# Attention's last four steps: transposes into the banks of the scores, and one sum a step later

## The chip, the cores and the metric

The kernel runs on one core of a Trainium2 chip. The metric is the device time of one execution in microseconds (us); before the change it is 531.19 us, the median of three runs (530.88 to 531.22). Engines are named as in the profile: PE (matrix products and transposes), PEld (its weight loads), DVE (vector), ACT (scalar), POOL (GpSimd), SP (which issues most DMAs). PE's results go to PSUM, which the program lays out as eight banks of 128 x 512 float32 values.

## The reference

Two stages follow each other: an attention with a bias that a small network computes from positions, and a layer with three weight matrices whose products are joined by a maximum.

```
scores = q @ k.T / sqrt(64) + bias(positions)        # 4 batches, 8 heads, 576 x 576
attn   = exp(scores - max); attn = attn / (sum(attn) + 1e-9)
x      = (attn @ v) as 2304 tokens x 512
h      = max(x @ w1, x @ w2, x @ w3)                 # 2304 x 768
out    = h @ w_out                                   # 2304 x 512
```

## The kernel before

The order of instructions on every engine is the order in which the program writes them; nothing is reordered later, and the framework only adds the waits between engines. It does so by tiles: two accesses of one tile by different engines may be given a wait, accesses of different tiles are not.

**The attention's steps.** The attention works through 72 steps (`NSTEP`), each 128 rows of scores for two heads. A step `n` goes through a pipeline that is five steps deep. In step `n` PE makes the scores (`front`, tiles `s`, two tiles of two banks each), DVE adds the bias and takes the maximum (`shift`), and ACT makes the exponentials (`expo`, tile `e`). Two steps later POOL multiplies `e` by the reciprocal of the row sums (`norm`, line 332; the reciprocal `rc` is DVE's, line 328, once for two steps). Four steps later (`LAG`) `flip` lets PE transpose `e` in pieces of 64 columns into PSUM: sixteen transposes go to the two one-bank tiles `tp..._0` and `tp..._1` (`ps_t`, tag `t`, two buffers, so one step's pair fills both), and two more go to the tile `lp` (one bank, one buffer), one of them first of all and one last. Then `empty` copies: ACT takes `tp..._0` and `lp` (line 470), DVE takes `tp..._1` (line 474), into the SBUF tile `et`. The products of `et` with the values (line 400) go to the one-bank tile `pv` (one buffer); DVE copies a finished `pv` to the tiles `xb` at the start of the next step (`split_x`, line 420).

**The drain.** In steps 72 to 75 (`n >= NSTEP`) no new scores are made, and the steps only finish what is in the pipeline: four calls of `flip`, those of the last pair of units, whose names are `tp_5` to `tp_8` in the program. There the spare time of DVE and ACT serves the next stage: `late_x` is cut into pieces, and the main loop lets each step do one piece for `vector` and one for `scalar`. Its pieces are sums and differences of blocks of `xb` (`sum`, on DVE, line 553; t3 in two halves, then t2), roundings of such a block (`high`, a cast on ACT, line 578) and remainders (`low`, on DVE or on POOL, line 553). In step 75, and after it, t4 and the last products follow; the last ones go to the tile `pvlast`, which takes a buffer of tag `t`.

**The second stage** (`moe`, line 653) begins as soon as PE has made the last products of the attention. It is a long row of products of 128x128 by 128x384 (lines 665 to 667).

The PSUM pool in this stretch has four banks of tag `s` (two buffers of two banks), two of tag `t`, one of `lp` and one of `pv`.

Of the kernel before, what the change touches and what calls it, by code (L numbers as in the profile page):

```python
# [19 lines left out]
def kernel(  # L20
# [17 lines left out]
    NTQ = S // 128  # L38
    LB = 128 * NTQ
# [10 lines left out]
    def ps_s(name, tag="s"):  # L50
        return psums[-1].tile([128, 2, 512], F32, tag=tag, bufs=2, name=name)
# [7 lines left out]
    def ps_t(name):  # L59
        return psums[-1].tile([128, 512], F32, tag="t", bufs=2, name=name)  # L60
# [148 lines left out]
    NSTEP = len(sched)  # L209
    LAG = 4  # L210
# [4 lines left out]
    def step_of(pair, y):  # L215
        return ORDERS[units[2 * pair][0] % 2][y]

    class Attention:
# [122 lines left out]
        def flip(self, n):  # L341
            pair, y = fronts[n]
            which, t = step_of(pair, y)
            pool, e2 = self.pool, self.st.pop(n)["e"]
            if y == MIX:
                self.group(2 * pair + 1, 1)
                parts = [(2 * pair, GW, 0, LEFT), (2 * pair + 1, GW, LEFT, LEFT)]
            else:
                un = 2 * pair + which
                if y in (0, 2, 7):  # L350
                    self.group(un, int(y == 2))
                parts = [(un, 128 * (t % 2), 0, 128)]
            lp = psums[-1].tile([128, 128], F32, tag="l", bufs=1, name=f"lp{pair}_{y}")
            tps = [ps_t(f"tp{pair}_{y}_{r}") for r in range(2)]
            blocks = [(2 * c + h, S * h + 128 * c + LEFT * h) for h in range(2) for c in range(NTQ)]

            def turn(r, to, k0):
                p = slice(64 * r, 64 * r + 64)
                return nc.tensor.transpose(to, e2[p, k0:k0 + 128], ident[p, p])  # L359

            a = turn(0, lp[:, 0:64], LB)
            for i, (o, k0) in enumerate(blocks):
                turn(1, tps[1][:, 64 * o:64 * o + 64], k0)
                turn(0, tps[0][:, 64 * o:64 * o + 64], k0)
            b = nc.tensor.nop()
            tc.add_manual_dep(b.ins, a.ins.name, mybir.DependencyInfo(
                mybir.DependencyClass.Sync, mybir.DependencyReason.DATA), reason="two row tiles write one bank")
            turn(1, lp[:, 64:128], LB)
            out = []
            for r in range(2):  # L370
                src = tps[r].rearrange("p (c h q) -> p c h q", c=NTQ, h=2)
                un, c0 = parts[r if y == MIX else 0][0:2]
                c0 += 0 if y == MIX else 64 * r
                out.append([(self.et[un][0][:, :, :, c0:c0 + 64], src)])
            out.append([(self.et[un][1][:, c0:c0 + w], lp[:, r:r + w]) for un, c0, r, w in parts])
            return out
# [746 lines left out]
    with tc.manual_schedule():  # L1123
# [4 lines left out]
        n = 0  # L1128
# [147 lines left out]
        x0 = Blocks(0, xa, xa)  # L1276
# [14 lines left out]
        def late_x():  # L1291
            yield "vector"
            x0.sum("t3", 0)
            yield "vector"
            x0.sum("t3", 1)
            x0.high("t3")
            x0.sum("t2")
            yield "scalar"
            x0.high("b21")
            yield "vector"  # L1300
            x0.low("b21", nc.gpsimd)
            yield "scalar"
            x0.high("t2")
            yield "vector"
            x0.low("t3")
            yield "scalar"
            x0.high("b22")
            yield "vector"
            x0.low("b22", nc.gpsimd)

        BEHIND = {3: 1, 5: 1, 7: 2, 11: 1, 13: 2, 15: 1}
        ex, lx = Stream(early_x()), Stream(late_x())
        while n < NSTEP + LAG:
            more = []
# [72 lines left out]
```

## Time and profile before

| what | value |
|---|---|
| median of three runs | 531.19 us (530.88 to 531.22) |
| the profiled execution's own time | 531.41 us |
| its span (first to last instruction) | 529.6 us |
| PE busy | 520.9 us, 98% of the span |
| DVE, ACT, POOL busy | 437.1, 358.0, 261.6 us |
| DMA | 78.66 MB, mean 149 GB/s |
| drain of the attention, first transpose to first product of the next stage | 249.55 to 261.05 us |

The span is 1.8 us shorter than the execution that it is part of. A row of the timeline gives the start and the length of an instruction or of a run of equal ones, and in brackets how long its engine had been idle and which instruction ended that. PE's matrix products are pipelined: several are under way at once, so a row of several products ends later than the last one starts, and PE counts as busy in short gaps between two starts.

### The profile page before, as it was taken

How to read it: one execution, taken by the hardware profiler on the slowest of the kernel's cores; microseconds unless marked ns; L12 is line 12 of the kernel's file. 1: busy time of each engine (PE TensorE's matmuls, PEld its weight loads, DVE VectorE, ACT ScalarE, POOL GpSimd, SP SyncE). 2: the span in 40 equal slices, each digit the busy share in tenths (PEclk: the TensorE clock that was granted, in tenths of full speed). 3: DMA queues.
4: the chain of work that ended last, by engine and by line, in shares of the span. 5: the costliest groups of instructions: out<-in, count | busy, mean ns of one | idle time of the engine just before them, and what ended most of it. 6: DMA issues, size and time to landing. Idle time of an engine off the chain costs nothing.

```text
span 529.6 us, 13653 instructions
## 1 busy us (share of the span) xinstructions
PE 520.9 (98%) x5175; PEld 434.1 (82%) x5175; DVE 437.1 (83%) x931; ACT 358.0 (68%) x803; POOL 261.6 (49%) x291
## 2 busy tenths in 40 slices
PE   8999999999999999999999999999999999999997
PEld 4454667676767676767799999999999999999997
DVE  7999979898989898988898998648887346898883
ACT  7998989998989999988685343442434325455552
POOL 0003878678878897987600074645665525300000
PEclk9999999999999999999999999999999999999999
DMA  6895998533675183211102225342275440756642
GB/s 188 256 340 150 318 286 239 163 108 109 214 227 152 25 244 120 68 24 38 67 0 81 79 70 179 131 160 79 80 251 170 145 141 11 249 178 179 198 143 80
DMA packets 73474, 78.66 MB, mean 149 GB/s; under 512 B 23168, under 2 KB 54528, under 8 KB 73408
## 3 DMA queue, kind: packets, MB, share of 16 engines
q1 hardware_dynamic: 73264, 77.49, 47.0%
q8 instruction: 41, 0.67, 0.5%
q10 hardware_dynamic: 144, 0.29, 0.2%
q14 instruction: 25, 0.20, 0.1%
HBM read 49.56 MB, written 27.94 MB: 146 GB/s over the span
## 4 chain that ended last, share of the span: by engine, by line
PE 90%; DVE 5%; ACT 2%; issue 1%; DMA 1%; DVEq 0%; ACTq 0%
PE pv L400 16%; PE p L667 12%; PE p L666 12%; PE p L665 12%; PE s L294 11%; PE tp L359 6%; PE p_o L1048 4%; PE p_o L1047 4%; PE p_o L1046 4%; PE bp L138 4%; DVE hid L116 3%; ACT e L318 2%; PE lp L359 2%; PE s L284 2%; DVE sn L304 1%
## 5 line engine op out<-in xcount | busy, mean ns | idle before, releaser
L332 POOL TENSOR_SCALAR e<-e,rc 128x576 f32<-128x576 f32 x144 | 111.6, 794 | 28.2 <-DVE rc L328 22.9
L304 DVE CUSTOM_DVE_ANT_0 sn<-s,bias 128x576 f32<-128x576 f32 x144 | 103.2, 754 | 22.1 <-PE lp L359 12.1
L318 ACT ACTIVATE e<-sn,nm 128x576 f32<-128x576 f32 x144 | 111.4, 780 | 4.6 <-DVE nm L304 4.4
L400 PE MATMUL pv<-et,vt 128*64 128x320 f32 (+1 forms) x496 | 74.0, 419 | 0.1
L359 PE MATMUL tp<-ident,e 64*128 64x64 f32 x1152 | 53.2, 224 | 0.5 <-ACT et L470 0.3
L474 DVE COPY et<-tp 128x512 f32<-128x512 f32 x72 | 49.3, 685 | 2.6 <-PE tp L359 2.5
L470 ACT COPY et<-tp 128x512 f32<-128x512 f32 x72 | 41.8, 581 | 12.4 <-PE lp L359 11.1
L294 PE MATMUL s<-kh,qh 64*128 64x288 f32 x240 | 48.3, 343 | 1.6 <-DVE nm L304 1.5
L359 PEld LDWEIGHTS tp<-ident,e 64*128 64x128 f32 x1152 | 47.4, 139 | 0.9 <-ACT et L470 0.4
L294 PEld LDWEIGHTS s<-kh,qh 64*128 64x128 f32 x240 | 28.1, 185 | 22.0 <-DVE nm L304 9.6
L400 PEld LDWEIGHTS pv<-et,vt 128*64 128x64 f32 x496 | 30.2, 136 | 17.8 <-issue 1.6
L707 ACT COPY u<-p 128x384 f32<-128x384 f32 x26 | 12.5, 481 | 43.4 <-PE p L667 43.3
L138 PE MATMUL bp<-hid,w2s 128*32 128x79 f32 (+51 forms) x640 | 40.4, 390 | 1.2 <-DVE hid L116 0.8
L294 PE MATMUL s<-kl,qh 64*128 64x288 f32 x240 | 41.0, 296 | 0.0
L294 PE MATMUL s<-kh,ql 64*128 64x288 f32 x240 | 39.9, 291 | 0.0
L116 DVE TENSOR_SCALAR hid<-sm,bp 128x528 f32<-128x528 f32 (+17 forms) x108 | 39.2, 447 | 0.0
L714 ACT COPY u<-p 128x384 f32<-128x384 f32 x26 | 12.5, 480 | 38.3 <-PE p L667 38.2
L138 PEld LDWEIGHTS bp<-hid,w2s 128*32 128x32 f32 x640 | 19.2, 109 | 22.9 <-issue 15.9
L553 POOL TENSOR_TENSOR ws<-wr 128x256 f32<-128x256 f32 x16 | 13.5, 844 | 47.9 <-DVE wl L553 47.5
L359 PE MATMUL lp<-ident,e 64*128 64x64 f32 x144 | 33.1, 230 | 1.1 <-ACT et L470 0.4
L553 DVE TENSOR_TENSOR q<-p,u 128x384 f32<-128x384 f32 x36 | 19.9, 554 | 15.7 <-ACT u L714 13.2
L359 PEld LDWEIGHTS lp<-ident,e 64*128 64x128 f32 x144 | 19.8, 137 | 13.6 <-issue 8.2
(236 smaller groups left out, 1627.5 us busy)
## 6 DMA issues: line engine op xcount, KB each, us to landing
bias_d<-bs SPq DMA_DIRECT2D x36, 295.5 KB, 5.1
w<-in_moe_w_dram SPq DMA_DIRECT2D x36, 256.0 KB, 3.1
bias<-bias_d SPq DMA_DIRECT2D x15, 576.0 KB, 5.5
h_d<-ht SPq DMA_DIRECT2D x18, 384.0 KB, 3.2
hin<-h_d SPq DMA_DIRECT2D x16, 384.0 KB, 4.4
qr<-in_qd_dram SPq DMA_DIRECT2D x16, 288.0 KB, 4.5
kr<-in_kd_dram SPq DMA_DIRECT2D x16, 288.0 KB, 5.3
vt<-in_v_dram SPq DMA_DIRECT2D x32, 128.0 KB, 3.3
```

The lines of the kernel that those rows point to most:

```text
L116: marks["hid"] = nc.vector.tensor_scalar(out=h[:, 0:n], in0=wl[:, 0:n], scalar1=k["bp"][:, m:m + 1], scalar2=0.0, op0=ALU.add, op1=ALU.max)
L138: nc.tensor.matmul(bp[32 * c:32 * c + 32, o:o + w], lhsT=w2s, rhs=src, start=True, stop=True)
L294: nc.tensor.matmul(ss[h][:, x, 0:HALF], lhsT=u[q][p, 128 * t:128 * t + 128], rhs=u[k][p, cols], start=(j == 0), stop=(j == len(terms) - 1))
L304: nc.vector.tensor_tensor_reduce(out=sn.rearrange("p (a b) -> p a b", a=2), in0=st["s"][h][:, :, 0:HALF], in1=bt.rearrange("p (a b) -> p a ...
L318: nc.scalar.activation(st["e"][:, S * h:S * h + S], sn, ACTF.Exp, scale=-1.0, bias=nm, accum_out=self.sm[:, x:x + 1])
L332: nc.gpsimd.tensor_scalar(out=e, in0=e, scalar1=self.rc[:, x:x + 1], scalar2=1.0, op0=ALU.mult, op1=ALU.mult)
L359: return nc.tensor.transpose(to, e2[p, k0:k0 + 128], ident[p, p])
L400: nc.tensor.matmul(pv[p], lhsT=w, rhs=x, start=(c == 0), stop=(c == NTQ))
L474: nc.vector.tensor_copy(*x)
L665: nc.tensor.matmul(o, lhsT=hi[:, c], rhs=h[:, j], start=first and j == 0, stop=False, **on)
L666: nc.tensor.matmul(o, lhsT=hi[:, c], rhs=l[:, j], start=False, stop=False, **on)
L667: nc.tensor.matmul(o, lhsT=lo[:, c], rhs=h[:, j], start=False, stop=last and j == 1, **on)
```

## The change

Two things are changed. In the four calls of `flip` whose step is one of the last four (`drain`), the two tiles of tag `t` are replaced by one tile of two banks from `ps_s`, of the tag that the scores use; its two buffers are taken in turn. In the same calls the first transpose into `lp` stands after the first eight of the other transposes (`NTQ` blocks of two) and no longer ahead of all. And in `late_x` the sum of t2 moves from the piece of the second half of t3 to the next piece for `vector`, behind the low part of b21.

```
@@ flip @@
             lp = psums[-1].tile([128, 128], F32, tag="l", bufs=1, name=f"lp{pair}_{y}")
-            tps = [ps_t(f"tp{pair}_{y}_{r}") for r in range(2)]
+            drain = n >= NSTEP - LAG
+            if drain:
+                tps = ps_s(f"tp{pair}_{y}")
+                tps = [tps[:, r] for r in range(2)]
+            else:
+                tps = [ps_t(f"tp{pair}_{y}_{r}") for r in range(2)]
...
-            a = turn(0, lp[:, 0:64], LB)
             for i, (o, k0) in enumerate(blocks):
+                if i == (NTQ if drain else 0):
+                    a = turn(0, lp[:, 0:64], LB)
                 turn(1, tps[1][:, 64 * o:64 * o + 64], k0)
                 turn(0, tps[0][:, 64 * o:64 * o + 64], k0)
@@ late_x @@
             x0.high("t3")
-            x0.sum("t2")
             yield "scalar"
             x0.high("b21")
             yield "vector"
             x0.low("b21", nc.gpsimd)
+            x0.sum("t2")
             yield "scalar"
             x0.high("t2")
```

**DVE in the drain.** The rows are DVE's program order from the copy of the `pv` of step 71 to the difference `t3l`. `tp_5` to `tp_7` are the transposed tiles of steps 72 to 74 (in the kernel before, the digit behind is the bank), `t_0` from `xb,xb` is the sum of t3, `t_0` from `t_0,xb` that of t2, and the brackets name the engines whose semaphore the instruction waits for. Before:

```order
L420 COPY xb_2_1179<-pv_0_5143 128x256
L474 COPY et_1_5234<-tp_5_1_5277 128x8x64 [waits PE_49]
L328 RECIPROCAL rc_5308<-sm_5213 128x4 [waits Activation_49,Pool_49]
L553 TENSOR_TENSOR t_0_5153<-xb_0_1172,xb_0_1169 128x384
L553 TENSOR_TENSOR t_0_5315<-t_0_5153,xb_0_1170 128x768 [waits DVE_49]
L474 COPY et_1_5234<-tp_6_1_5321 128x8x64 [waits PE_49]
L420 COPY xb_1_1175<-pv_1_5300 128x192 [waits PE_49]
L420 COPY xb_2_1179<-pv_1_5300 128x64 x2
L474 COPY et_0_5357<-tp_7_1_5360 128x8x64 [waits PE_49]
L553 TENSOR_TENSOR t3l_5390<-t_0_5153,t3h_5313 128x768 [waits DVE_49,Activation_49]
```

And after the change, the same stretch:

```order
L426 COPY xb_2_1179<-pv_0_5143 128x256
L480 COPY et_1_5234<-tp_5_5276 128x8x64 [waits Activation_49]
L328 RECIPROCAL rc_5307<-sm_5213 128x4 [waits Pool_49]
L559 TENSOR_TENSOR t_0_5153<-xb_0_1172,xb_0_1169 128x384
L480 COPY et_1_5234<-tp_6_5317 128x8x64 [waits Activation_49]
L559 TENSOR_TENSOR t_0_5348<-t_0_5153,xb_0_1170 128x768 [waits DVE_49]
L426 COPY xb_1_1175<-pv_1_5299 128x192 [waits PE_49]
L426 COPY xb_2_1179<-pv_1_5299 128x64 x2
L480 COPY et_0_5355<-tp_7_5357 128x8x64 [waits Activation_49]
L559 TENSOR_TENSOR t3l_5387<-t_0_5153,t3h_5312 128x768 [waits DVE_49]
```

The sum of t2 has changed places with the copy out of `tp_6`, and every copy out of a `tp` now names ACT where it named PE.

**PE in step 72.** The rows are PE's from the first transpose of the step to the first product into the next `pv`; before:

```order
L359 MATMUL lp_5_5275<-ident,e_5088 128x64 [waits Activation_49,Pool_49]
L359 MATMUL tp_5_1_5277<-ident,e_5088 128x64 [waits PE_49]
L359 MATMUL tp_5_0_5276<-ident,e_5088 128x64 [waits DVE_49]
...
L359 MATMUL lp_5_5275<-ident,e_5088 128x64 [waits PE_49]
L400 MATMUL pv_1_5300<-et_1_5112,vt_4917 64x320 [waits DVE_49,PE_49]
```

And after:

```order
L364 MATMUL tp_5_5276<-ident,e_5088 128x64 [waits DVE_49,Pool_49]
L364 MATMUL tp_5_5276<-ident,e_5088 128x64 x7
L364 MATMUL lp_5_5275<-ident,e_5088 128x64 [waits Activation_49,Pool_49]
L364 MATMUL tp_5_5276<-ident,e_5088 128x64 x8
L364 MATMUL lp_5_5275<-ident,e_5088 128x64 [waits PE_49]
L406 MATMUL pv_1_5299<-et_1_5112,vt_4917 64x320 [waits DVE_49,PE_49]
```

The wait for ACT, which is for the `lp` of the step before, stands behind eight transposes now, and the wait for DVE stands ahead of all and is for scores that DVE has read.

## Rows read from the trace of the kernel before

**Rows 1.** The page: each engine's busy time, share of the span, instructions

```profile
PE 520.9 (98%) x5175; PEld 434.1 (82%) x5175; DVE 437.1 (83%) x931; ACT 358.0 (68%) x803; POOL 261.6 (49%) x291
```

**Rows 2.** Busy time by stretches: stretch, length, engines, PEclk, DMA share, GB/s

```profile
262.00:290.00 28.00, 28.00 (x164) 28.00 (x163) 25.99 (x34) 19.99 (x34) 0.00 (x0) 1.00 0.12 38
```

**Rows 3.** Timeline of PE, the drain: start, length, engine, line, what, idle before

```profile
249.55 0.24 PE L359 MATMUL lp<-ident,e 64*128 64x64 f32 x1 [0.43 <-ACT et L470]
...
250.00 0.71 PE L359 MATMUL tp<-ident,e 64*128 64x64 f32 x15 [0.17 <-DVE et L474]
...
250.64 1.84 PE L400 MATMUL pv<-et,vt 128*64 128x320 f32 x12
252.41 0.27 PE L359 MATMUL lp<-ident,e 64*128 64x64 f32 x1
...
253.11 0.76 PE L400 MATMUL pv<-et,vt 128*64 128x320 f32 x4
...
254.34 0.27 PE L359 MATMUL lp<-ident,e 64*128 64x64 f32 x1
...
255.18 1.83 PE L400 MATMUL pv<-et,vt 128*64 128x320 f32 x12
...
257.65 0.76 PE L400 MATMUL pv<-et,vt 128*64 128x320 f32 x4
...
258.77 1.92 PE L400 MATMUL pvlast<-et,vt 128*64 128x256 f32 x16
...
261.05 0.44 PE L665 MATMUL p<-b11h,wh 128*128 128x384 f32 x1
```

**Rows 4.** Timeline of DVE, the drain

```profile
249.86 0.41 DVE L420 COPY xb<-pv 128x256 f32<-128x256 f32 x1
250.69 0.69 DVE L474 COPY et<-tp 128x512 f32<-128x512 f32 x1 [0.42 <-PE tp L359]
251.30 0.17 DVE L328 RECIPROCAL rc<-sm 128x4 f32<-128x4 f32 x1
251.39 0.53 DVE L553 TENSOR_TENSOR t<-xb,xb 128x384 f32<-128x384 f32 x1
251.95 1.38 DVE L553 TENSOR_TENSOR t<-t,xb 128x768 f32<-128x768 f32 x1
...
254.46 0.62 DVE L420 COPY xb<-pv 128x192 f32<-128x192 f32 x3 [0.53 <-PE pv L400]
...
255.70 2.29 DVE L553 TENSOR_TENSOR t3l<-t,t3h 128x768 fp32r<-128x768 f32 x1
...
260.42 0.95 DVE L553 TENSOR_TENSOR t<-xb,t 128x768 f32<-128x768 f32 x1
```

**Rows 5.** Timeline of ACT, the drain

```profile
249.01 0.40 ACT L470 COPY et<-lp 128x64 f32<-128x64 f32 x2
...
251.07 0.57 ACT L470 COPY et<-tp 128x512 f32<-128x512 f32 x1
...
251.95 0.83 ACT L578 CAST t3h<-t 128x768 fp32r<-128x768 f32 x1
252.69 0.83 ACT L578 CAST b21h<-xb 128x768 fp32r<-128x768 f32 x1
253.42 0.58 ACT L470 COPY et<-tp 128x512 f32<-128x512 f32 x1
253.90 0.27 ACT L470 COPY et<-lp 128x128 f32<-128x128 f32 x1
...
257.75 0.59 ACT L470 COPY et<-tp 128x512 f32<-128x512 f32 x1 [1.12 <-PE tp L359]
```

**Rows 6.** Timeline of POOL, the drain

```profile
247.73 2.92 POOL L332 TENSOR_SCALAR e<-e,rc 128x576 f32<-128x576 f32 x4 [1.24 <-DVE rc L328]
251.63 3.76 POOL L332 TENSOR_SCALAR e<-e,rc 128x576 f32<-128x576 f32 x4 [0.99 <-DVE rc L328]
255.35 1.83 POOL L553 TENSOR_TENSOR b21l<-xb,b21h 128x768 fp32r<-128x768 f32 x1
```

More of the change, by code (lines that the diff above doesn't have):

```diff
@@ L353, in flip @@
             lp = psums[-1].tile([128, 128], F32, tag="l", bufs=1, name=f"lp{pair}_{y}")
-            tps = [ps_t(f"tp{pair}_{y}_{r}") for r in range(2)]
+            drain = n >= NSTEP - LAG
+            if drain:
+                tps = ps_s(f"tp{pair}_{y}")
+                tps = [tps[:, r] for r in range(2)]
+            else:
+                tps = [ps_t(f"tp{pair}_{y}_{r}") for r in range(2)]
             blocks = [(2 * c + h, S * h + 128 * c + LEFT * h) for h in range(2) for c in range(NTQ)]
@@ L359, in turn @@
                 return nc.tensor.transpose(to, e2[p, k0:k0 + 128], ident[p, p])
-            a = turn(0, lp[:, 0:64], LB)
             for i, (o, k0) in enumerate(blocks):
+                if i == (NTQ if drain else 0):
+                    a = turn(0, lp[:, 0:64], LB)
                 turn(1, tps[1][:, 64 * o:64 * o + 64], k0)
@@ L1296, in late_x @@
             x0.high("t3")
-            x0.sum("t2")
             yield "scalar"
@@ L1301, in late_x @@
             x0.low("b21", nc.gpsimd)
+            x0.sum("t2")
             yield "scalar"
```

## The prediction

> **What bounds the kernel now.** The page comes first: PE is busy for 98% of the span [rows 1], so a change helps only where PE stands, and hurts only where it makes PE stand. Next the table by stretches, for what follows the attention: from 262 to 290 us PE is busy for 28.00 of 28.00 us, at a granted clock of 1.00 [rows 2], and the same view of the later stretches up to 500 us reads alike. So whatever moves the first product of the next stage, at 261.05, moves the end by as much; nothing behind it takes a gain or a loss back. Then the timeline of PE in the drain [rows 3]: PE stands for 0.43 us until ACT has copied the old `lp` and, two transposes later, for 0.17 us until DVE has copied the old `tp`. After that it hardly stands. The timelines of the other three engines [rows 4, 5, 6] show who is close behind PE there.
>
> From rows 3 I take PE's own pace: 1.77 us from the first of twelve `pv` rows to the next transposes (250.64 to 252.41), 1.23 us for eight (253.11 to 254.34), 0.70 us from the first transpose of an unstalled step to its products (252.41 to 253.11), and 1.12 us from the last eight `pv` rows to `pvlast` (257.65 to 258.77).
>
> **What the new banks give.** In step 72 the transposes no longer wait for DVE's copy. The wait for the old `lp` remains: ACT ends that copy at 249.01 + 0.40 = 249.41 [rows 5] and PE's `lp` began at 249.55, 0.14 later [rows 3]. It now holds back only the second eight transposes. In the kernel before, fifteen of them took from 250.00 to the products at 250.64; half of them take some 0.41, so PE would be ready at 249.96, 0.68 earlier. But the products go to the single `pv` bank, which DVE empties until 249.86 + 0.41 = 250.27 [rows 4]. With 0.08 for the wait the products begin at 250.35: a gain of 0.29 us, no more. At its own pace PE would begin step 73 at 252.12, its products at 252.82, step 74 at 254.05.
>
> **What the new tile costs.** The program's order shows that each DVE copy out of `tp` now waits for ACT, and the ACT instruction that reads the same tile is ACT's own copy of the other half. In the kernel before DVE copied at 250.69, ahead of ACT at 251.07 [rows 4, 5]. ACT's place doesn't change, since two exponentials and a small sum stand ahead of its copy. So DVE now starts at 251.07 + 0.57 + 0.03 = 251.67, that is 0.98 later (0.03 is what ACT takes to follow DVE: t3 ends at 251.39 + 0.53 = 251.92 and the cast of it starts at 251.95). Behind that copy in DVE's queue stand the reciprocal (now 252.28) and t3 (now 252.37 to 252.90). Two engines wait for these:
>
> - ACT's cast of t3, then its cast of b21, then its copies of step 73. They start at 251.95, 252.69, 253.42 and 253.90 [rows 5]; each is 0.98 later, the `tp` copy from 254.40 to 254.98, the `lp` copy to 255.15.
> - POOL's normalization, whose four pieces started 0.16 us behind the reciprocal [rows 4, 6]. They now start at 252.61; undisturbed, four take 2.92 instead of 3.76 [rows 6], and with t3 beside the first they end at some 255.68. No transpose is late by that.
>
> Step 74's transposes start at 254.05, and the second eight wait for the `lp` copy: 255.15 + 0.14 = 255.29, so PE is ready for the next `pv` at 255.70. Before, these products began at 255.18, just behind DVE's copies out of `pv` (254.46 + 0.62 = 255.08). Those copies are now later still. DVE's copy of step 73 waits for ACT's: 255.01 to 255.70. Then comes the moved sum of t2, from 255.63, and only then the copies out of `pv`.
>
> **The moved sum.** Its own length is 0.95 us, as the sum of equal shape at 260.42 shows; at 251.95 it took 1.38, with POOL's pieces beside it [rows 4, 6]. Its length in the new place is the unknown. The lower end is 0.95, the upper end a wait for all of POOL's b21 remainder (1.83, [rows 6]) with the sum behind it. Three rows tell how the two engines meet. At 251.95 DVE waited while POOL finished one piece, and went ahead of the next. The difference at 255.70 took 2.29 and ended at 257.99, 0.81 after POOL's remainder (255.35 + 1.83 = 257.18): again DVE stood for one POOL instruction and then ran at its own speed. So what matters is which is first. POOL's last piece ends at 255.68 and its remainder follows; DVE asks at 255.63, in time by 0.05. I take the lower end: the sum ends at 255.63 + 0.95 = 256.58.
>
> The Trainium skill says the same of this pair (SBUF — State Buffer, section SBUF: two separate sides): the shared port is an exclusive lock for a whole instruction, and the loser blocks. A split of bandwidth instead would stretch the sum to between 1.38 and 2.29 and give 534.0 to 534.9; the rows of 251.95 and 255.70 speak for the lock.
>
> **The sum.** The copies out of `pv` run from 256.50 to 257.12, and the last `pv` begins at 257.22 (0.10 behind, as before): 2.04 late. PE is at step 75 at 257.22 + 1.77 = 258.99, at its products at 259.69. ACT's copy starts 0.10 behind those (257.75 against 257.65, [rows 3, 5]), 259.79 to 260.38, and DVE's only then, 260.41 to 261.10. ACT and DVE are free by then: the cast of t2 starts at 256.61, ACT's copy of step 74 ends near 257.95, DVE's near 258.67, and the difference of t3 behind it near 259.54. `pvlast` needs both copies: at PE's pace it would begin at 259.69 + 1.12 = 260.81, but it waits until 261.10 + 0.06 = 261.16. Against 258.77 that is 2.39 us, of which 2.04 come from the queue around the moved sum and the rest from the two copies one after the other at the end. The tail of DVE behind `pvlast` shifts by no more than PE, so the next stage stays as it is.
>
> The profiled execution takes 531.41 us; 531.41 + 2.39 = 533.80. The runs' median lies 0.22 lower, so the forecast is 533.6 us.
>
> The Trainium skill speaks against any cost here (PSUM — Partial Sum Buffer, section Specifications (TRN2)): ScalarE and VectorE can read PSUM side by side at full rate when they use different banks. The two halves lie in two banks, so the chip would allow it; the rows of step 72, where DVE's copy (250.69 to 251.38) and ACT's (from 251.07) overlap, agree. By that rule the time would be that of the second rival below, and it doesn't apply if the program itself makes one wait for the other.
>
> **The rivals.**
>
> - *POOL is first.* If the remainder of b21 takes the port before t2, DVE stands until 255.66 + 1.83 = 257.49 and the sum ends near 258.30 (0.81 behind, as in the row of 255.70). All that follows is 1.7 later: 535.3 us. For it speaks the margin of 0.05 us, less than the latencies that I added up; against it, that DVE twice went ahead of a POOL instruction that was just starting.
> - *Not slower: the copies in effect run side by side.* If DVE's wait were met early, DVE would copy in step 72 before its reciprocal, which with t3 would stay at 251.30 and 251.39. It would copy step 73 from 252.89 to 253.58, t2 would run from 253.50 to 254.88 (at its old length of 1.38), the copies out of `pv` from 254.80 to 255.42, and the last `pv` would begin at 255.52, 0.34 late: 531.5 us, no change. It is decided at ACT's copy of step 72: ended by 250.6 it costs nothing, and all of its lateness beyond that counts. Against it: the wait in the program, and ACT's end at 251.64, which nothing in the change makes earlier.
> - *Faster.* All that PE loses to the old banks is the 0.68 us of step 72; with a free `pv` bank as well it would come through, and the time would be 530.5 us. That is still within 0.2%, so a clear gain would need a wait that I don't see.
>
> **How the numbers follow.** Forecast 0.61 (own range 533.0 to 534.4, from the latencies of some 0.05 us that add up over a dozen steps), POOL first 0.24 (534.9 to 535.7), no change 0.12, a clear gain 0.03. A measurement tells a difference of 0.2%, some 1.06 us, from none. So slower 0.85, same 0.12, faster 0.03. The range of 532.6 to 535.7 leaves out the last two cases and little else.
>
> **What would show it.** In the new profile: transposes of step 72 from near 249.1, its products near 250.35; DVE's copies each behind ACT's, the first near 251.67; ACT's `lp` copy of step 73 ending near 255.15 with PE waiting for it; the sum of t2 from near 255.63, of 0.95 us (or some 2.7 if POOL is first); the last `pv` near 257.2; `pvlast` near 261.2 behind DVE; the next stage near 263.4 and no idle PE in it. The forecast is wrong if DVE copies beside ACT, or if the copies out of `pv` start before 256 us.

## The result, and the profile after

The changed kernel takes 536.59 us (median of six runs, 536.24 to 538.54) against 531.13 us of the kernel before on the same chip: 1.0108 times as long, 95% interval 1.0098 to 1.0118. That is 5.46 us more, where 2.39 were forecast; the time lies 0.9 us above the range. The profiled execution took 537.24 us; its span is 535.5 us against 529.6. The next stage starts 6.09 us later, at 267.14 against 261.05, and from there both kernels run alike: PE is busy for all of the first 253 us in either. So the whole loss lies ahead of that stage.

The timeline of PE in the drain answers to [rows 3]; columns as there.

```profile
248.98 0.46 PE L364 MATMUL tp<-ident,e 64*128 64x64 f32 x8
249.48 0.24 PE L364 MATMUL lp<-ident,e 64*128 64x64 f32 x1
...
250.35 1.83 PE L406 MATMUL pv<-et,vt 128*64 128x320 f32 x12 [0.30 <-DVE xb L426]
...
255.21 0.24 PE L364 MATMUL lp<-ident,e 64*128 64x64 f32 x1 [0.62 <-ACT et L476]
...
258.81 3.47 PE L406 MATMUL pv<-et,vt 128*64 128x320 f32 x12 [3.02 <-issue]
262.20 0.79 PE L364 MATMUL tp<-ident,e 64*128 64x64 f32 x9
...
263.36 1.00 PE L406 MATMUL pv<-et,vt 128*64 128x320 f32 x4
...
264.83 1.95 PE L406 MATMUL pvlast<-et,vt 128*64 128x256 f32 x16
...
267.14 0.44 PE L671 MATMUL p<-b11h,wh 128*128 128x384 f32 x1
```

Step 72 starts 0.57 earlier, and its products 0.29 earlier than the 250.64 of before. Of both, 0.07 is no gain: this execution runs that much ahead before the change can act, as the first row of DVE below shows (249.79 against 249.86 in [rows 4]). The loss is in two places: PE stands for 3.02 us ahead of the last `pv`, and then the same twelve products take 3.39 us to the next transposes, where they took 1.76, from 255.18 in [rows 3] to this row of the kernel before:

```profile
256.94 0.27 PE L359 MATMUL lp<-ident,e 64*128 64x64 f32 x1
```

For the first place look at DVE; its timeline answers to [rows 4].

```profile
249.79 0.41 DVE L426 COPY xb<-pv 128x256 f32<-128x256 f32 x1
251.60 0.69 DVE L480 COPY et<-tp 128x512 f32<-128x512 f32 x1 [1.40 <-ACT et L476]
252.21 0.17 DVE L328 RECIPROCAL rc<-sm 128x4 f32<-128x4 f32 x1
252.30 0.52 DVE L559 TENSOR_TENSOR t<-xb,xb 128x384 f32<-128x384 f32 x1
254.94 0.69 DVE L480 COPY et<-tp 128x512 f32<-128x512 f32 x1 [2.12 <-ACT et L476]
255.54 2.63 DVE L559 TENSOR_TENSOR t<-t,xb 128x768 f32<-128x768 f32 x1
258.10 0.61 DVE L426 COPY xb<-pv 128x192 f32<-128x192 f32 x3
...
264.08 0.69 DVE L480 COPY et<-tp 128x512 f32<-128x512 f32 x1 [2.97 <-ACT et L476]
```

Every copy out of `tp` in the drain now ends an idle time with ACT's name behind it, and the sum of t2, the row of 128x768, takes 2.63 us instead of the 0.95 that was forecast. The timelines of ACT and of POOL, for [rows 5, 6], show who it waited for.

```profile
251.00 0.57 ACT L476 COPY et<-tp 128x512 f32<-128x512 f32 x1
...
254.32 0.58 ACT L476 COPY et<-tp 128x512 f32<-128x512 f32 x1
254.80 0.27 ACT L476 COPY et<-lp 128x128 f32<-128x128 f32 x1
...
263.46 0.59 ACT L476 COPY et<-tp 128x512 f32<-128x512 f32 x1 [3.04 <-PE tp L364]
```

```profile
252.57 3.02 POOL L332 TENSOR_SCALAR e<-e,rc 128x576 f32<-128x576 f32 x4 [2.00 <-DVE rc L328]
255.56 1.79 POOL L559 TENSOR_TENSOR b21l<-xb,b21h 128x768 fp32r<-128x768 f32 x1
```

ACT's copies end 0.03 ahead of DVE's (251.57 and 251.60, 264.05 and 264.08). POOL's remainder of b21 runs from 255.56 to 257.35, undisturbed, and t2 ends at 258.17, 0.82 behind it: DVE stood for the whole POOL instruction and then ran at its own speed.

The table by stretches has the second place: stretch, length, busy time of PE, PEld, DVE, ACT, POOL (in brackets the number of instructions), then PE's granted clock, the DMA share and GB/s.

```profile
255.80:257.00 1.20, 0.00 (x0) 0.00 (x0) 1.20 (x1) 0.00 (x0) 1.20 (x1) 1.00 0.00 0
257.00:258.80 1.80, 0.00 (x0) 0.02 (x1) 1.71 (x4) 0.59 (x1) 0.36 (x1) 0.52 0.00 0
258.80:260.00 1.20, 1.19 (x6) 0.67 (x8) 0.44 (x1) 1.20 (x4) 0.00 (x0) 0.50 0.00 0
260.00:262.00 2.00, 2.00 (x10) 0.69 (x6) 1.11 (x2) 0.42 (x1) 1.50 (x1) 0.50 0.00 0
...
263.00:264.00 1.00, 1.00 (x13) 0.61 (x12) 0.00 (x0) 0.54 (x2) 0.00 (x0) 0.56 0.00 0
264.00:265.00 1.00, 1.00 (x10) 0.37 (x8) 0.72 (x2) 0.22 (x2) 0.00 (x0) 1.00 0.00 0
...
267.00:290.00 23.00, 23.00 (x134) 22.86 (x133) 20.78 (x27) 17.16 (x28) 0.00 (x0) 1.00 0.08 24
```

PE ran at a granted clock of 1.00 (2.4 GHz), did nothing from 255.80, and soon after 257.00 the clock fell to 0.50 (1.2 GHz). It stayed there until almost 264, through the last twelve products and the transposes of step 75.

| from, to | before | after | difference | forecast |
|---|---|---|---|---|
| start of the last `pv` | 255.18 | 258.81 | +3.63 | +2.04 |
| to the transposes of step 75 | 1.76 | 3.39 | +1.63 | 0 |
| to the products of step 75 | 0.71 | 1.16 | +0.45 | 0 |
| to `pvlast` | 1.12 | 1.47 | +0.35 | +0.35 |
| to the next stage | 2.28 | 2.31 | +0.03 | 0 |
| sum | | | +6.09 | +2.39 |

So 1.59 us are missing in the start of the last `pv`, and 2.08 in PE's pace behind it.

### The profile page after: what moved, and what is told of

It reads as the page before. It is cut to its first block, busy times and chain, and to the rows that moved or that the text cites. A ratio compares the mean times of both kernels' runs of the same rounds, so it can differ in the third digit from the quotient of the medians.

```text
span 535.5 us, 13651 instructions
## 1 busy us (share of the span) xinstructions
PE 523.1 (98%) x5175; PEld 435.5 (81%) x5175; DVE 437.0 (82%) x931; ACT 357.5 (67%) x803; POOL 260.3 (49%) x291
## 4 chain that ended last, share of the span: by engine, by line
PE 90%; DVE 5%; issue 2%; ACT 1%; DMA 1%; DVEq 0%
PE pv L406 16%; PE p L673 12%; PE p L672 12%; PE p L671 12%; PE s L294 12%; PE tp L364 6%; PE p_o L1053 4%; PE p_o L1054 4%; PE p_o L1052 4%; PE bp L138 4%; DVE hid L116 3%; PE lp L364 2%; PE s L284 1%; DVE sn L304 1%; DMA sm<-in_small_dram 1%
## 5 line engine op out<-in xcount | busy, mean ns | idle before, releaser
L332 POOL TENSOR_SCALAR e<-e,rc 128x576 f32<-128x576 f32 x144 | 110.4, 783 | 29.3 <-DVE rc L328 24.0
L406 PE MATMUL pv<-et,vt 128*64 128x320 f32 (+1 forms) x496 | 75.9, 428 | 3.3 <-issue 3.0
L559 POOL TENSOR_TENSOR wl<-ws,wh 128x256 fp32r<-128x256 f32 x26 | 25.8, 1019 | 10.3 <-ACT wh L763 10.3
```

Of the source, the lines that this page charges most:

```text
L332: nc.gpsimd.tensor_scalar(out=e, in0=e, scalar1=self.rc[:, x:x + 1], scalar2=1.0, op0=ALU.mult, op1=ALU.mult)
L406: nc.tensor.matmul(pv[p], lhsT=w, rhs=x, start=(c == 0), stop=(c == NTQ))
L559: eng.tensor_tensor(out=out, in0=f(a), in1=f(b), op=op)
```

## Experiments

My theory after this result has four parts: the one tile makes the two copies serial; that delay puts the moved sum on the path; POOL took the port that it shares with DVE ahead of the sum; and the long stand halved PE's clock. The rivals: one half of the change alone costs it all; the banks themselves, and not the tile, hold DVE back; POOL is served first whenever both engines want the port. Each ratio is to the kernel before on the same chip.

**The halves.** First the new tile alone, with t2 back in its old place (the new place of `lp` stays):

```diff
             x0.high("t3")
+            x0.sum("t2")
...
             x0.low("b21", nc.gpsimd)
-            x0.sum("t2")
```

> The changed kernel with the sum of t2 back ahead of DVE's copy of step 73; the new tile and the place of `lp` stay. Theory (three losses in a row: DVE's copies behind ACT's in one tile, then t2 behind POOL's b21 remainder, then the clock at half after a stand of PE of 3 us): t2 runs from about 253.4, while POOL still normalizes, the copies out of `pv` follow DVE's copy of step 73 (still near 254.9 to 255.6) and the last `pv` begins near 256.3; PE stands some 0.5 us there, the clock stays at 1.00, and only the two serial copies ahead of `pvlast` are left: 532.6 us, slower than before by some 0.3%. Rival (the new tile alone makes the loss): 536 to 537 us. Rival (the moved sum alone makes it): 531 us.

532.96 us, ratio 1.0027 (1.0018 to 1.0037): +1.49 us, 0.4 above what I expected. Timeline of DVE:

```profile
251.76 0.69 DVE L480 COPY et<-tp 128x512 f32<-128x512 f32 x1 [1.40 <-ACT et L476]
...
253.01 1.38 DVE L559 TENSOR_TENSOR t<-t,xb 128x768 f32<-128x768 f32 x1
255.09 0.69 DVE L480 COPY et<-tp 128x512 f32<-128x512 f32 x1 [0.70 <-ACT et L476]
255.70 0.61 DVE L426 COPY xb<-pv 128x192 f32<-128x192 f32 x3
```

In its old place t2 lies inside the time that DVE waits for ACT; that wait is 2.12 us in the changed kernel and 0.70 here. The moved sum is what leaves this cover.

Then the moved sum alone, with the old tiles and the old order of the transposes:

```diff
-            if drain:
-                tps = ps_s(f"tp{pair}_{y}")
-                tps = [tps[:, r] for r in range(2)]
-            else:
+            if True:
                 tps = [ps_t(f"tp{pair}_{y}_{r}") for r in range(2)]
...
-                if i == (NTQ if drain else 0):
+                if i == 0:
```

> The kernel before with the sum of t2 moved and nothing else. Theory: DVE copies step 73 on its own near 253.2, t2 asks for the port near 253.9 and waits for one normalization of POOL at most; the last `pv` begins 0.2 to 0.9 us late, the clock stays at 1.00: 531.3 to 532.1 us. Rival (the moved sum alone makes the loss, wherever the transposes go): 535 us or more.

531.61 us, ratio 0.9997 (0.9987 to 1.0007): no cost. So neither half has the 5.46 us, and the sum is dear only behind the late copy.

**Tile or bank.** Two separate tiles in place of one, in steps 72 and 74 one bank of each buffer of the scores, in steps 73 and 75 the old tag:

```diff
-            if drain:
-                tps = ps_s(f"tp{pair}_{y}")
-                tps = [tps[:, r] for r in range(2)]
+            if drain and n % 2 == 0:
+                tps = [ps_s(f"tp{pair}_{y}_{r}")[:, 0] for r in range(2)]
```

> The changed kernel with two tiles instead of one: steps 72 and 74 take one bank of each of the two score tiles, steps 73 and 75 take tag `t`; t2 stays where the change put it. Theory (the wait comes from the one tile, not from the banks): every DVE copy out of `tp` waits for PE again, step 72's gain of 0.3 us remains, t2 costs some 0.2 us in its new place: as the kernel before within 0.2%, 531.0 to 531.8 us. Rival (transposes into the scores' banks cost by themselves): 533 us or more.

531.36 us, ratio 1.0000 (0.9991 to 1.0010). DVE again copies ahead of ACT, and t2, still in its new place, no longer stands behind a late copy; the last `pv` begins at 254.98, 0.10 behind the copies out of the one before it, after a stand of PE of 0.33 us:

```profile
249.79 0.68 DVE L479 COPY et<-tp 128x512 f32<-128x512 f32 x1
...
252.54 0.69 DVE L479 COPY et<-tp 128x512 f32<-128x512 f32 x1 [1.05 <-PE tp L363]
253.15 1.20 DVE L558 TENSOR_TENSOR t<-t,xb 128x768 f32<-128x768 f32 x1
254.27 0.61 DVE L425 COPY xb<-pv 128x192 f32<-128x192 f32 x3
```

It is the shared tile, then, and not the banks of the scores. The same with t2 in its old place:

> As the run with two tiles, and the sum of t2 back in its old place: what the banks alone can give. Theory: step 72's products begin 0.29 us earlier (the `pv` bank holds back the rest of 0.68) and the last `pv` 0.3 us earlier: 0.1 to 0.3 us faster than before, too little to be told from it. Rival (the transposes' banks are worth the whole 0.68 us): 530.5 to 530.8 us against 531.2.

531.29 us, ratio 0.9999 (0.9987 to 1.0011). The new banks are worth nothing that can be measured, and no version that beats the kernel before came out of this.

Last, the one tile, with DVE's copies written ahead of ACT's in the last four steps:

```diff
+                drain = n >= NSTEP
+                if drain:
+                    self.split_x()
+                    for x in tp1:
+                        nc.vector.tensor_copy(*x)
                 for x in tp0 + ([] if shared else left):
...
-                for x in tp1 + (left if shared else []):
+                for x in [] if drain else tp1 + (left if shared else []):
```

> The changed kernel with the order of the two copies out of the one tile turned in the last four steps: the copy out of `pv` and DVE's copy out of `tp` are written ahead of ACT's, so that ACT waits for DVE. Theory (the wait hurts because DVE, which is early, stands behind ACT, which is late): DVE copies step 72 near 250.3, t3 is back at 251.4, t2 follows the copy of step 73 near 253.6, the last `pv` begins near 255.4 instead of 258.8; only the two serial copies ahead of `pvlast` remain, some 0.5 us: 531.7 to 532.3 us, clock at 1.00. Rival (one tile for two engines costs the same whoever goes first): 536 us.

532.17 us, ratio 1.0018 (1.0004 to 1.0032). Now ACT waits. In ACT's timeline the copies of steps 73 to 75:

```profile
253.52 0.59 ACT L481 COPY et<-tp 128x512 f32<-128x512 f32 x1 [0.23 <-DVE et L479]
...
255.71 0.58 ACT L481 COPY et<-tp 128x512 f32<-128x512 f32 x1 [0.30 <-DVE et L479]
...
258.48 0.58 ACT L481 COPY et<-tp 128x512 f32<-128x512 f32 x1 [1.29 <-DVE et L479]
```

The copies are serial in whichever order they are written; with DVE first most of the loss goes, since DVE is the engine that comes early. (In two of the ten runs the clock fell: 532.92 us at a mean of 0.997 and 535.40 at 0.994. The profiled one is at 1.00, so what PE did in them is not known.)

**The port.** POOL's remainder of b21 is made to depend on t2:

```diff
+                tc.add_manual_dep(i.ins, behind.ins.name, mybir.DependencyInfo(
+                    mybir.DependencyClass.Sync, mybir.DependencyReason.DATA), reason="a port that two engines share")
...
-            x0.low("b21", nc.gpsimd)
-            x0.sum("t2")
+            i = x0.sum("t2")
+            x0.low("b21", nc.gpsimd, behind=i)
```

> The changed kernel with one more dependency: POOL's remainder of b21 waits for DVE's sum of t2, so that POOL can't be first at the port. Theory: t2 takes 0.95 us from about 255.55 instead of 2.63, the last `pv` begins near 257.15, PE stands 1.4 us instead of 3.0, the clock stays at 1.00: 533.6 us, what the forecast was. Rival (the long row of t2 isn't POOL's doing, or the stand comes from elsewhere): 536 to 537 us, as the changed kernel.

534.98 us, ratio 1.0064 (1.0042 to 1.0085), 1.4 above what I expected. The sum did as forecast: it took 0.95 us, and in PE's timeline the last `pv` begins at 256.96, 1.85 earlier than in the changed kernel (0.17 of it because this execution runs that much ahead from the start, so 1.68 for the port).

```profile
256.96 2.75 PE L406 MATMUL pv<-et,vt 128*64 128x320 f32 x12 [1.33 <-issue]
259.64 0.79 PE L364 MATMUL tp<-ident,e 64*128 64x64 f32 x9
```

But these products take 2.68 us to the transposes, and the stretches show why:

```profile
257.00:258.00 1.00, 1.00 (x8) 0.67 (x10) 0.28 (x1) 1.00 (x4) 1.00 (x1) 0.87 0.00 0
258.00:259.00 1.00, 1.00 (x8) 0.43 (x4) 1.00 (x2) 0.58 (x1) 0.64 (x2) 0.50 0.00 0
...
261.00:262.00 1.00, 1.00 (x8) 0.36 (x6) 0.48 (x1) 0.65 (x2) 0.00 (x0) 0.92 0.00 0
```

After a stand of 1.33 us the clock fell to 0.50 when PE was already at work again. It fell in three of the four runs (mean 0.997, 0.997 and 0.994); the fourth took 534.39 us at 1.000, 0.8 more than I expected at a full clock, and I have no cause for that.

How narrow the order at the port is, a small POOL instruction ahead of the remainder tells:

```diff
+    pause = const.tile([128, 64], F32, name="pause")
...
             yield "vector"
+            nc.gpsimd.memset(pause, 0.0)
             x0.low("b21", nc.gpsimd)
```

> The changed kernel, with one small extra instruction on POOL (a 128x64 tile set to zero, which nothing reads) between its last piece of the normalization and the remainder of b21, so that POOL asks for the port a little later; nothing else is changed and nothing is left out. If the port goes to whichever of the two engines is there first, and DVE lost by the few hundredths of a us that its copy before t2 still ran, t2 now goes ahead, takes 0.95 us, and the remainder of b21 starts when t2 has ended; the last products then begin near 257.0, PE stands for some 1.3 us, and the time is that of the kernel in which b21 waits for t2, 534.5 to 535.2 us. If POOL is served first whenever both want the port (or its pause is too short to matter), t2 takes 2.6 us again, the last products begin near 258.8, and the time is 536.2 to 537.0 us.

534.67 us, ratio 1.0051 (1.0034 to 1.0069). Timelines of DVE and of POOL:

```profile
255.08 0.69 DVE L481 COPY et<-tp 128x512 f32<-128x512 f32 x1 [2.12 <-ACT et L477]
255.69 0.95 DVE L560 TENSOR_TENSOR t<-t,xb 128x768 f32<-128x768 f32 x1
```

```profile
255.68 0.14 POOL L1307 MEMSET pause<- 128x64 f32 x1
255.79 2.52 POOL L560 TENSOR_TENSOR b21l<-xb,b21h 128x768 fp32r<-128x768 f32 x1
```

An instruction of 0.14 us turned the order around: t2 takes 0.95 and the remainder 2.52, which is 0.7 more than its 1.8. POOL is not preferred; who is there first goes first. The runs also show the clock from the side. Three, at a mean granted clock of 1.000, took 533.42 to 533.56 us; three at 0.997 took 534.67 to 535.17. (A seventh took 535.68 at 1.000, for which I have no cause.) The same program is some 1.6 us longer where the clock fell.

**The clock.** PE is kept at work during the stand of the changed kernel, by 20 transposes of the identity that nobody reads, behind step 74's:

```diff
+            if n == NSTEP - 2:
+                idle = ps_t("idle")
+                for _ in range(FILLERS):
+                    nc.tensor.transpose(idle[:, 0:128], ident, ident)
...
+    FILLERS = 20
```

> The changed kernel with twenty more transposes of the identity on PE, behind those of step 74, into a bank that nothing reads: they fill part of the stand of 3 us. Theory (the fall of the clock is a loss of its own): the last `pv` begins near 258.8 as in the changed kernel, but the granted clock stays at 1.00 and the twelve `pv` rows take 1.77 us instead of 3.4; 534.5 to 535.0 us, some 1.7 to 2.1 us below the changed kernel. Rival (the products are slow for another reason, such as the banks): the same 536 to 537 us, or more if the transposes last longer than the stand.

535.46 us, ratio 1.0069 (1.0053 to 1.0086), 0.5 above what I expected. In PE's timeline the pace behind the stand is that of before, 1.76 us to the transposes, and the granted clock is 1.00 throughout; t2 still took 2.66 us, as the rows of DVE and of POOL show that follow those of PE.

```profile
256.02 2.40 PE L378 MATMUL idle<-ident 128*128 128x128 f32 x20
259.14 1.83 PE L410 MATMUL pv<-et,vt 128*64 128x320 f32 x12 [0.71 <-issue]
260.90 0.52 PE L364 MATMUL tp<-ident,e 64*128 64x64 f32 x9
```

```profile
255.85 2.66 DVE L563 TENSOR_TENSOR t<-t,xb 128x768 f32<-128x768 f32 x1
```

```profile
255.87 1.82 POOL L563 TENSOR_TENSOR b21l<-xb,b21h 128x768 fp32r<-128x768 f32 x1
```

Last, both misses are taken away at once: b21 behind t2, and 10 such transposes.

> The changed kernel with POOL's remainder of b21 behind t2, and ten more transposes of the identity on PE behind those of step 74, into a bank that nothing reads. Theory: with POOL behind, t2 takes 0.95 us, and with PE busy the granted clock stays at 1.00, so what is left is the forecast of the changed kernel without its two misses: last `pv` near 257.1, `pvlast` near 261.1, 533.4 to 533.9 us. Rival (the queue around t2 costs more than the forecast had it): 534.5 us or more at a clock of 1.00.

533.51 us, ratio 1.0038 (1.0023 to 1.0053), with the last `pv` straight behind the idle transposes:

```profile
255.94 1.31 PE L378 MATMUL idle<-ident 128*128 128x128 f32 x10
257.35 1.84 PE L410 MATMUL pv<-et,vt 128*64 128x320 f32 x12
```

That is the forecast of 533.6 us, and the three runs of the pause at full clock agree with it.

In the eight runs with these transposes the mean clock was 0.999 to 1.000; in all six of the changed kernel it was 0.997 or 0.994. A long stand is not the only thing that goes with a fallen clock: 4 of 54 runs of the kernel before, whose profile shows no such stand in the drain, were at 0.997 too and took 532.23 to 533.38 us. What PE did in those is not on record.

## Why the prediction was wrong

The medians, each less its own kernel before, give the parts of the 5.46 us. The profiles give them once more: there the start of the next stage is counted from DVE's copy out of the `pv` of step 71, which takes out how far an execution ran ahead (before, 261.05 - 249.86 = 11.19).

| what is in the kernel | over before | adds | in the profile, over before |
|---|---|---|---|
| one tile, t2 in its old place | +1.49 | 1.5: serial copies | +1.53 |
| and t2 moved, ahead of POOL, PE kept busy | +2.14 | 0.7: the sum loses its cover | +2.40 |
| and POOL first | +3.99 | 1.9: DVE waits for the port | +4.11 |
| and PE idle (the change) | +5.46 | 1.5: half clock | +6.16 |

The intervals of the four ratios are 0.5 to 0.9 us to either side, so by the times alone the 0.7 is not told from nothing; the profiles have 0.87 there.

Right were the direction and the first two parts:

- *New banks.* PE was free at 250.05, 0.30 ahead of its products (forecast 249.96), and was held at the single `pv` bank; the products began at 250.35, as forecast. To the hundredth that is luck: DVE's copy out of `pv` ended at 249.79 + 0.41 = 250.20, and PE followed 0.15 later, not 0.08. Of the 0.29 us gained, 0.22 is the change's.
- *New tile.* DVE's first copy began at 251.60 (forecast 251.67), t3 at 252.30 (252.37), ACT's `lp` copy of step 73 ended at 255.07 (255.15), DVE's second copy ran from 254.94 to 255.63 (255.01 to 255.70). Each is ahead by the 0.07 or so that the whole execution is ahead.
- *Two copies ahead of `pvlast`.* The term of 0.35 came out as 0.35.

Two steps failed.

**"In time by 0.05. I take the lower end."** The times were right, the comparison was not. In the new profile t2's row starts at 255.54 and POOL's four pieces end at 252.57 + 3.02 = 255.59: the same 0.05 apart as forecast, and the sum took 2.63 in place of 0.95 all the same. I had read the start of DVE's row as its claim on the port. But the copy ahead of t2 was still running, until 254.94 + 0.69 = 255.63, and by then POOL's last piece had been over for 0.04. The forecast's own times read in this way, 255.70 for DVE's copy and 255.68 for POOL's last piece, would have had POOL first by 0.02. A second profile agrees: with PE kept busy the copy ended at 255.93 and POOL's pieces at 255.91, and POOL was first, though t2's row again starts 0.02 ahead of POOL's. With the pause DVE's copy ended at 255.77 and the pause at 255.82, and DVE was first; there both readings say so. These are hundredths of a us in a few profiles, so that the end of the instruction ahead decides is likely, not shown.

This is the rival "POOL is first", with the price of 1.7 given there; its own time, 535.3, is what the run with PE kept busy measured, 535.46. Its chance of 0.24 was too low: the margin was within the latencies that I had added up, and the row of 251.95 that spoke against it was no tie, since DVE was already waiting there when POOL's piece ended. The runs that were not profiled fit POOL first as well: at a mean clock of 0.997 the changed kernel took 536.24 to 536.60 us in all four, the two kernels with t2 first 534.67 to 535.17.

The Trainium skill (SBUF — State Buffer, section SBUF: two separate sides) has whichever starts first keep the port for the whole instruction. The two orders, 2.63 beside 1.79 in the changed kernel and 0.95 beside 2.52 with the pause, agree.

**"PE is at step 75 at 257.22 + 1.77 = 258.99, at its products at 259.69."** The sum carried 1.77 us and 0.70 us of [rows 3] over to a PE that had stood, and no term, rival or end of the range had a slower PE. By the forecast itself PE would be ready at 255.70 and get its bank at 257.22, a stand of 1.5 us where before there was hardly any. Behind stands of 1.33 us (the kernel with b21 behind t2) and 3.02 us (the change) the clock was at 0.50; by the medians the first cost 3.51 - 2.14 = 1.4 us and the second 5.46 - 3.99 = 1.5. With PE kept at work the clock stayed at 1.00. Either step by itself would have left the time in the range: 535.46 us with POOL first and the clock kept at 1.00, 534.98 with t2 first and the clock fallen in three of four runs. In four of the six runs of the changed kernel the mean clock is 0.997, in the profiled one and one other 0.994, so the 2.08 us of the profile is more than the median run lost.

The Trainium skill (TensorE: Matmul & The Clock Gate, Part 1: The HAM clock gate) says that an idle PE is throttled to half its clock; 0.50 in the stretches above agrees with it.

Of the rivals, "Not slower" fell with the first row of DVE's copies. "Faster" stays without support: with the tile split and t2 back, the gain of step 72 can't be told from nothing.

## What to carry to other kernels

When a step is moved, ask what it was hiding behind in its old place: t2 stood inside a wait of its engine, and the same change that lengthened the wait took the sum out of it. Two halves of one tile that two engines read are copied one after the other, in program order, even if they lie in different banks; two tiles cost nothing here. Where a forecast makes the engine that bounds the kernel stand, for 1.33 and 3.02 us here, it needs a term for its clock. Where two engines reach a shared port within some hundredths of a us of each other, both orders need their full price and about even chances, and the end of the instruction ahead has to be compared, not only the start of a row.

## What the runs showed of the hardware

- PE's clock need not fall within the stand. After 1.33 us without work it fell when the next products were some 0.8 us old (0.87 over 257 to 258 us is half speed for the last 0.26, and the products began at 256.96), and in other runs of the same program it did not fall at all (three with the pause, at a mean of 1.000).
- Transposes of the identity, 20 in 2.40 us, kept the granted clock at 1.00.
- A POOL instruction of 0.14 us was worth some 2 us (536.59 against 534.67 us) by the order of two engines at one port. In the two profiles where POOL won, t2's row started 0.02 us before POOL's, but DVE's copy ahead of it ended 0.04 and 0.02 us after POOL's last piece.
